# Tile 0 loaded in two halves on two queues, K of two tiles projected together, LayerNorm of tiles 2 and 3 skewed: an attention and gated-MLP kernel

## The chip, the cores and the metric

The kernel runs on one core of one Trainium2 chip. The metric is the device time of one execution in microseconds (us). Executions of one kernel spread by about 1 us here, so every verdict rests on several rounds in which two kernels run in turn on the same chip. The span that a profile shows is about 2 us shorter than the timed run.

A core has engines with instruction queues of their own: TensorE (PE, with PEld for its weight loads), VectorE (DVE), ScalarE (ACT), GpSimd (POOL) and SyncE (SP), which in this kernel only issues transfers. Transfers ("DMA") are issued on SP's, ACT's or POOL's queue.

## The reference

```python
x = A_x                                   # 1 x 2048 x 640, bf16
xn = _layernorm(x)
return x + _A_ref(xn, A_wqkv, A_wo) + _B_ref(xn, B_w_gate, B_w_up, B_w_down)

# A: q, k, v = split(xn @ wqkv), 32 heads of 20; each position attends to 8 earlier
#    positions 2 apart; softmax; the weighted sum of v; @ wo
# B: ((xn @ w_gate) * (xn @ w_up)) @ w_down, inner width 1536
```

## The kernel before

Rows are worked in 16 tiles of 128 (tile t holds rows 128t to 128t+127), the width of 640 in 5 chunks of 128. A small scheduler, `op(engine, fn, r=, w=)`, appends to the engine's queue in program order and derives all semaphore waits from what is read and written. So **the order of the calls is the order of each engine's queue**, and an instruction that waits holds up all that stand behind it.

The first four tiles are normalised and transposed on TensorE through PSUM. From tile 4 on SP issues a transposing DMA. The parts that the change touches:

```python
# loads: SP's queue unless eng says otherwise
op("act", ... ACT.Sqrt ..., name="sqrt_preload")
x_load(1, "act")
x_load(0)
for c in range(NCH):
    wqkv_load(0, c)                 # Q weights by chunk, 160 KB each
x_load(2)
x_load(3)
for c in range(NCH):
    wqkv_load(1, c)                 # K weights by chunk
...                                 # tiles 4 to 12

def ln_aggr(t):                     # cut: bn_aggr on DVE, then the square root on ACT
    op("dve", ... bn_aggr(mv, st) ...)
    op("act", ... activation(sd, mv[:, 1:2], ACT.Sqrt, bias=EPSC[:, 0:1]) ...)

def ln_sums(t, k):                  # tile 1's statistics, all on ACT: sum, sum of squares, square root
    ...

def ln_apply(t, between=None):      # cut: reciprocal and (x - mean) * rstd on DVE
    ...
    if t >= NTP:                    # NTP = 4
        op("sp", lambda e: e.dma_start_transpose(o, xs), ...)

def ln_copy(t, only=(0, 1, 2)):     # PSUM to XNT after the transposes: (engine, from chunk, to chunk)
    parts = ((("act", 0, 1), ("dve", 1, 3), ("act", 3, NCH)), (("dve", 0, 2), ("act", 2, NCH)), ...)[t]
    ...

warm(10)                            # dummy matmuls of 512 columns
ln_stats_a(0)
ln_stats_b(0)
ln_sums(1, 0)
ln_aggr(0)
ln_sums(1, 1)
ln_sums(1, 2)
ln_apply(0)
ln_pe(0)                            # five transposes
ln_copy(0, (0, 1, 2))
ln_apply(1)
warm(2, TS)
...
# projections of tiles 0 and 1: Q(0), Q(1), K(0), K(1), chunk by chunk; part_evac moves the result to SBUF on ACT
order = ((0, 0), (0, 1), (1, 0), (1, 1)) if t0 < 4 else ((0, 0), (1, 0), (0, 1), (1, 1))
at = {(0, 0): (3, lambda: tr(1)), (1, 0): (3, lambda: tr(2)), (1, 1): (4, lambda: tr(3))}
for which, dt in order:
    ...
    proj_tile(which, t, b, bm, (2 * which + t) * TS, at.get((which, t)))
    part_evac(which, t, 1, 0, 4, b, 0)
    tp += 1.4
    ...
    ln_pace(tp)                     # one more tile's LayerNorm each 1.45 us of planned time
```

Of the kernel before, what the change touches and what calls it, by code (L numbers as in the profile page):

```python
# [10 lines left out]
D = 640  # L11
NCH = 5
# [9 lines left out]
TS = 128  # L22
JB = 512
DHALF = D // 2
# [188 lines left out]
def build_kernel(nc, A_x, A_wqkv, A_wo, B_x, B_w_gate, B_w_up, B_w_down, out):  # L213
    K = Sched(nc)
    op = K.op
# [50 lines left out]
    XST = sb("XST", [128, NXS, D], at=a_log)  # L266
# [22 lines left out]
    xhbm = A_x[0]  # L289
    ohbm = out[0]  # L290

    def dma(o, i, r=(), w=(), name="", eng="sp", group=None):
        return op(eng, lambda e: e.dma_start(o, i), r=r, w=w, dma=True, name=name, group=group)
# [7 lines left out]
       r=[IDENT[:]], w=[IDENT[:]], name="ident")  # L301
# [7 lines left out]
    def x_load(t, eng="sp"):  # L309
        dma(XST[:, t % NXS, :], xhbm[t * TS:(t + 1) * TS, :], w=[XST[:, t % NXS, :]], name=f"xld{t}", eng=eng)  # L310
# [10 lines left out]
        dma(dst, wqkv_src[:, cs, g * D:(g + 1) * D], w=[dst], name=f"ld_wqkv{g}_{c}", eng=eng)  # L321

    op("act", lambda e: e.activation(DUM[:, 0:1], EPSC[:, 0:1], ACT.Sqrt), r=[EPSC[:]], w=[DUM[:]], name="sqrt_preload")
    x_load(1, "act")
    x_load(0)
    for c in range(NCH):
        wqkv_load(0, c)
    x_load(2)
# [11 lines left out]
    def late_loads():  # L340
        dma(MASK[0:128:4], MSK0[0:32], r=[MSK0[0:32]], w=[MASK[0:128:4]], name="mask")
        wqkv_load(2)
        for T, src in ((WG, B_w_gate), (WU, B_w_up)):
            for c in range(NCH):
                dma(T[:, c], src[c * 128:(c + 1) * 128, :], w=[T[:, c]], name="ld_w")

    def down_loads():
        dma(WD[:], B_w_down.rearrange("(c p) n -> p c n", p=128), w=[WD[:]], name="ld_wd")
# [15 lines left out]
    def ln_stats_a(t):  # L364
        if t >= NT:
            return
        x, st = XST[:, t % NXS, :], STATS[:, t % 2, 0:12]
        op("dve", lambda e: e.bn_stats(st[:, 0:6], x[:, 0:DHALF]), r=[x], w=[st], name=f"bna{t}")

    def ln_stats_b(t):  # L370
        if t >= NT:
            return
        x, st = XST[:, t % NXS, :], STATS[:, t % 2, 0:12]
        op("dve", lambda e: e.bn_stats(st[:, 6:12], x[:, DHALF:D]), r=[x], w=[("stb", t)], name=f"bnb{t}")

    def ln_aggr(t):
        if t >= NT:
            return
        st, mv, sd = STATS[:, t % 2, 0:12], MV[:, t, 0:2], SD[:, t, 0:1]
        op("dve", lambda e: e.bn_aggr(mv, st), r=[st, ("stb", t)], w=[mv], name=f"bnag{t}")  # L380
        op("act", lambda e: e.activation(sd, mv[:, 1:2], ACT.Sqrt, bias=EPSC[:, 0:1]), r=[mv, EPSC[:]], w=[("sd", t)],
           name=f"sd{t}")

    def ln_sums(t, k):
        x, xs, mv, sd = XST[:, t % NXS, :], XNS[:, t % NXN, :], MV[:, t, 0:2], SD[:, t, 0:1]
        nm, ss = mv[:, 0:1], mv[:, 1:2]
        if k == 0:
            op("act", lambda e: e.activation(xs, x, ACT.Copy, scale=-1.0 / D, accum_out=nm), r=[x], w=[xs, ("nm", t)], name=f"sta{t}")
        elif k == 1:
            op("act", lambda e: e.activation(xs, x, ACT.Square, bias=nm, accum_out=ss), r=[x, ("nm", t)], w=[xs, ("ss", t)],  # L390
               name=f"stq{t}")
        else:
            op("act", lambda e: e.activation(sd, ss, ACT.Sqrt, bias=EPSC[:, 0:1], scale=1.0 / D), r=[("ss", t), EPSC[:]],
               w=[("sd", t)], name=f"sd{t}")

    def ln_rstd(t):
        if t >= NT:
            return
        sd, rstd = SD[:, t, 0:1], SD[:, t, 1:2]
        op("dve", lambda e: e.reciprocal(rstd, sd), r=[("sd", t)], w=[("rstd", t)], name=f"rstd{t}")  # L400

    def ln_apply(t, between=None):
        if t >= NT:
            return
        x, xs, mv = XST[:, t % NXS, :], XNS[:, t % NXN, :], MV[:, t, 0:2]
        sd, rstd = SD[:, t, 0:1], SD[:, t, 1:2]
        op0 = ALU.add if t == 1 else ALU.subtract
        mean = ("nm", t) if t == 1 else mv
        if between is None:
            ln_rstd(t)  # L410
        else:
            between()
        for c0, c1 in ((0, 128), (128, D)) if t == 0 else ((0, D),):
            o, i = xs[:, c0:c1], x[:, c0:c1]
            op("dve", (lambda o, i: lambda e: e.tensor_scalar(o, i, mv[:, 0:1], rstd, op0=op0, op1=ALU.mult))(o, i),
               r=[i, mean, ("rstd", t)], w=[o], name=f"lnap{t}")
        if t >= NTP:
            o = XNT[:, :, t * TS:(t + 1) * TS]
            op("sp", lambda e: e.dma_start_transpose(o, xs), r=[xs], w=[o], dma=True, name=f"xT{t}")
        if t == 7:  # L420
            x_load(13)
            x_load2(14)
        if t == NT - 1:
            late_loads()

    def ln_pe(t):
        for c in range(NCH):
            o = tp_view(t, c, c + 1)[:, 0, :]
            i = XNS[:, t % NXN, c * 128:(c + 1) * 128]
            op("pe", (lambda o, i: lambda e: e.transpose(o, i, IDENT[:]))(o, i), r=[i, IDENT[:]], w=[o], name=f"tr{t}_{c}")  # L430

    def ln_copy(t, only=(0, 1, 2)):
        parts = ((("act", 0, 1), ("dve", 1, 3), ("act", 3, NCH)), (("dve", 0, 2), ("act", 2, NCH)), (("act", 0, NCH),),
                 (("act", 0, NCH),))[t]
        for k, (eng, c0, c1) in enumerate(parts):
            if k not in only:
                continue
            o = XNT[:, c0:c1, t * TS:(t + 1) * TS]
            tpv = tp_view(t, c0, c1)
            if eng == "dve":  # L440
                op("dve", (lambda o, i: lambda e: e.tensor_copy(o, i))(o, tpv), r=[tpv], w=[o], name=f"xntcp{t}_{c0}")
            else:
                op("act", (lambda o, i: lambda e: e.activation(o, i, ACT.Copy))(o, tpv), r=[tpv], w=[o],
                   name=f"xntcp{t}_{c0}")

    def warm(n, wide=JB):
        z = ZERO[:, 0:1].to_broadcast([128, wide])
        for _ in range(n):
            op("pe", lambda e: e.matmul(PS[:, 5, 0:wide], ZERO[:], z, start=True, stop=True), r=[ZERO[:]], w=[PS[:, 5, :]],  # L449
               name="warm")  # L450


    bank_ring = list(range(6))

    def bank():
        b = bank_ring.pop(0)
        bank_ring.append(b)
        return b
# [27 lines left out]
            op("pe", (lambda o, l, x, st, sp: lambda e: e.matmul(o, l, x, start=st, stop=sp))(o, l, x, st, sp),  # L486
               r=[l, x], w=[o], name=f"pp{which}_{m}_{t}_{c}")

    def proj_tile(which, t, b, bm, col, at=None):
        for c in range(NCH):  # L490
            if at is not None and at[0] == c:
                at[1]()
            for m in range(NCH):
                o = PS[:, b, m * TS:(m + 1) * TS] if m < 4 else PS[:, bm, col:col + TS]
                l, x = wcols(which, c, m), XNT[:, c, t * TS:(t + 1) * TS]
                st, sp = c == 0 and m in (0, 4), c == NCH - 1 and m in (3, 4)
                op("pe", (lambda o, l, x, st, sp: lambda e: e.matmul(o, l, x, start=st, stop=sp))(o, l, x, st, sp),  # L497
                   r=[l, x], w=[o], name=f"pp{which}_{m}_{t}_{c}")

# [204 lines left out]
                xr_load(t + NXR)  # L704


    warm(10)
    ln_stats_a(0)
    ln_stats_b(0)
    ln_sums(1, 0)  # L710
    ln_aggr(0)
    ln_sums(1, 1)
    ln_sums(1, 2)
    ln_apply(0)
# [8 lines left out]
        ln_stats_a(t + 1)  # L723
        ln_apply(t)

    def tr(t):
        ln_pe(t)
        if t != 2:
            ln_copy(t)
        ln_stats_a(t + 1)  # L730
        ln_stats_b(t + 1)
        ln_aggr(t + 1)
        if t == 2:
            ln_copy(t)
        if t < 3:
            ln_apply(t + 1)

    n_ln = [4]
    t_ln = [12.6]

    def ln_pace(t):
        while t_ln[0] <= t and n_ln[0] < NT:
# [5 lines left out]
            n_ln[0] += 1  # L748
            t_ln[0] += 1.45

    tp = 6.8
    for t0 in (0, 2, 4):
        bm = bank() if t0 == 4 else None
        if t0 == 2:
            bank_ring[:] = [5, 0, 6, 7, 2, 1, 3, 4]
            bm = bank()
        order = ((0, 0), (0, 1), (1, 0), (1, 1)) if t0 < 4 else ((0, 0), (1, 0), (0, 1), (1, 1))
        at = {(0, 0): (3, lambda: tr(1)), (1, 0): (3, lambda: tr(2)), (1, 1): (4, lambda: tr(3))}
        for which, dt in order:
            t = t0 + dt  # L760
            b = bank()
            if t0 == 0:
                if bm is None:
                    bm = bank()
                proj_tile(which, t, b, bm, (2 * which + t) * TS, at.get((which, t)))
            else:
                proj_part(which, t, (0, 1), b, 0)
                proj_part(which, t, (2, 3), b, 2 * TS)
                proj_part(which, t, (4,), bm, (2 * which + dt) * TS)
            part_evac(which, t, 1, 0, 4, b, 0)  # L770
            tp += 1.4
            if (which, dt) == (1, 1):
                for u in (0, 1):
                    part_evac(u, t0, 2, 4, 1, bm, 2 * u * TS)
            ln_pace(tp)
    bank_ring[:] = [6, 7, 2, 3, 4, 5, 0, 1]
    for g in range(5):
        b = bank()
# [187 lines left out]
```

## Time and profile before

| | |
|---|---|
| time, first three runs | 254.79 us median (254.24 to 255.25) |
| span of the profile | 252.5 us |
| TensorE busy | 99% |
| dummy matmuls | 1.00 to 5.45 us |
| first transpose of real data | 5.36 us |
| first projection matmul | 6.18 us |
| tile 0 landed / tile 1 landed | 3.03 / 3.72 us |
| Q weight chunks 2, 3, 4 (counted from 0) landed | 6.25, 6.63, 7.08 us |

The first lines of the page of before: the span, and for each engine the busy us, its share of the span and the number of instructions.

```profile
span 252.5 us, 3929 instructions
...
PE 249.1 (99%) x1623; PEld 149.3 (59%) x1623; DVE 214.7 (85%) x251; ACT 114.8 (45%) x204; POOL 35.9 (14%) x44
```

The chain that ended last, from the page of before, by engine:

```profile
PE 99%; DVE 0%; issue 0%
```

And the table of waits for TensorE, whole: engine, line and what it writes, what it waited for, us in total, times, longest.

```profile
PE PS L449 <- DVE EPSC L297: 1.0, 1, 1.0
```

All three say one thing: TensorE is the bound and never waits once it has started. Only two things can save time then: less TensorE work, or an earlier start of the useful work behind the dummies. How that start comes about is in the timeline of before (start us, duration, engine, line, operation, written<-read, form, count, and in brackets the idle time before it with what ended it):

```profile
3.06 0.49 DVE L368 BATCH_NORM_STATS2 STATS<-XST 128x6 f32<-128x320 bf16 x1 [1.75 <-DMA XST<-in_A_x_dram]
...
3.74 0.74 ACT L388 ACTIVATE XNS<-XST 128x640 bf16<-128x640 bf16 x1 [1.50 <-DMA XST<-in_A_x_dram]
...
3.98 0.21 DVE L380 BATCH_NORM_AGGREGATE MV<-STATS 128x2 f32<-128x12 f32 x1
...
4.48 0.28 ACT L381 ACTIVATE SD<-MV,EPSC 128x1 f32<-128x1 f32 x1
...
4.79 0.17 DVE L400 RECIPROCAL SD<-SD 128x1 f32<-128x1 f32 x1 [0.61 <-ACT SD L381]
4.99 0.64 DVE L415 TENSOR_SCALAR XNS<-XST,MV,SD 128x128 bf16<-128x128 bf16 x2
...
5.36 0.87 PE L430 MATMUL PS<-IDENT,XNS 128*128 128x128 bf16 x5
...
5.80 0.26 ACT L443 ACTIVATE XNT<-PS 128x128 bf16<-128x128 bf16 x1
...
6.18 1.04 PE L497 MATMUL PS<-XNT,WQKV 128*128 128x128 bf16 x15
```

The statistics of tile 0 are done at 4.19, but the square root (ACT L381) starts at 4.48, because ACT is still at tile 1's sum (L388). Ending times of the loads are read from the DMA semaphores in the trace.

### The profile page before, as it was taken

What the parts mean: (1) busy time and instruction counts of PE and PEld (TensorE: products, weight loads), DVE (VectorE), ACT (ScalarE), POOL (GpSimd) and SP (SyncE); (2) the same over time, 40 slices, a digit from 0 to 9 for tenths busy, and PEclk for the clock granted to TensorE, in tenths of its full rate; (3) what the DMA queues carried; (4) which work ended last, traced back from release to release, by engine and by line L of the source; (5) the groups of instructions that cost most, each with busy time, mean ns of one, the idle gap of its engine ahead of it and who ended that gap; (6) DMA issues with size and microseconds to landing.
All of it is one profiled execution on the core that took longest, in us unless ns stands there. A gap on an engine that the chain in (4) does not pass through costs nothing.

```text
span 252.5 us, 3929 instructions
## 1 busy us (share of the span) xinstructions
PE 249.1 (99%) x1623; PEld 149.3 (59%) x1623; DVE 214.7 (85%) x251; ACT 114.8 (45%) x204; POOL 35.9 (14%) x44
## 2 busy tenths in 40 slices
PE   8999999999999999999999999999999999999996
PEld 3999855555544444444444457764445777777775
DVE  4799999999999854999999974999999999993221
ACT  6577775555555557555555553135555112112000
POOL 1000001044515430003411110100000010111000
DMA  6969889956677471536379940393000021330511
GB/s 195 330 144 175 120 217 373 280 116 120 122 145 125 83 139 29 201 132 124 57 137 319 435 108 6 37 348 55 0 0 0 3 28 24 55 44 10 104 52 53
DMA packets 25649, 31.84 MB, mean 126 GB/s; under 512 B 9856, under 2 KB 22144, under 8 KB 25600
## 3 DMA queue, kind: packets, MB, share of 16 engines
q1 hardware_dynamic: 19104, 22.07, 28.4%
q0 software_dynamic: 6240, 9.31, 23.1%
q8 instruction: 12, 0.20, 0.3%
q10 hardware_dynamic: 288, 0.23, 0.3%
q14 instruction: 5, 0.04, 0.0%
HBM read 14.42 MB, written 4.59 MB: 75 GB/s over the span
## 4 chain that ended last, share of the span: by engine, by line
PE 99%; DVE 0%; issue 0%
PE PS L643 41%; PE PS L674 29%; PE PS L471 17%; PE PS L486 4%; PE PS L497 2%; PE PS L504 2%; PE PS L449 2%; PE PS L430 1%; DVE FOUT L688 0%; DVE ZERO L296 0%; DVE EPSC L297 0%
## 5 line engine op out<-in xcount | busy, mean ns | idle before, releaser
L643 PE MATMUL PS<-XNT,WG 128*128 128x512 bf16 x240 | 59.6, 379 | 0.0
L643 PE MATMUL PS<-XNT,WU 128*128 128x512 bf16 x240 | 59.6, 379 | 0.0
L610 DVE TENSOR_TENSOR PVB<-VO,ATB 128x10240 f16<-128x10240 bf16 x8 | 43.9, 5486 | 0.1
L471 PE MATMUL PS<-XNT,WQKV 128*128 128x512 bf16 x200 | 43.3, 379 | 0.0
L674 PE MATMUL PS<-WD,HT 128*128 128x320 bf16 (+2 forms) x300 | 43.2, 294 | 0.0
L643 PEld LDWEIGHTS PS<-XNT,WU 128*128 128x128 bf16 x240 | 23.5, 98 | 28.3
L643 PEld LDWEIGHTS PS<-XNT,WG 128*128 128x128 bf16 x240 | 23.5, 98 | 28.1
L645 ACT ACTIVATE USX<-PS 128x512 bf16<-128x512 f32 x48 | 28.7, 597 | 22.2 <-PE PS L643 21.2
L674 PEld LDWEIGHTS PS<-WD,HT 128*128 128x128 bf16 x300 | 28.7, 98 | 11.0
L471 PEld LDWEIGHTS PS<-XNT,WQKV 128*128 128x128 bf16 x200 | 23.5, 118 | 19.5
L605 DVE TENSOR_TENSOR PVB<-PVB 128x5120 f16<-128x5120 f16 (+1 forms) x16 | 34.5, 2154 | 0.3
L538 POOL DMA_DIRECT2D LOG<-PE x24 | 21.7, 931 | 59.6 <-DMA LOG<-PE 59.6
L645 ACT ACTIVATE HT<-PS 128x512 bf16<-128x512 f32 x36 | 21.5, 597 | 16.7 <-PE PS L643 16.7
L683 ACT ACTIVATE FACC<-PS 128x640 f16<-128x640 f32 x12 | 8.5, 704 | 45.4 <-PE PS L674 45.4
L674 PE MATMUL PS<-WO,VO 128*128 128x320 bf16 (+2 forms) x165 | 27.1, 295 | 0.0
L674 PEld LDWEIGHTS PS<-WO,VO 128*128 128x128 bf16 x165 | 15.9, 98 | 6.0
L527 DVE TENSOR_TENSOR PP<-QH,KH 128x2048 f16<-128x2048 bf16 x16 | 19.1, 1216 | 0.0
L527 DVE TENSOR_TENSOR TMP<-QH,KH 128x2048 f16<-128x2048 bf16 x16 | 19.0, 1216 | 0.0
L532 DVE TENSOR_TENSOR PP<-PP,TMP 128x4096 f16<-128x4096 f16 x8 | 18.3, 2288 | 0.2
L688 DVE TENSOR_TENSOR FOUT<-PS,XR 128x320 bf16<-128x320 f32 (+2 forms) x9 | 4.1, 454 | 16.6 <-PE PS L674 16.6
L698 POOL DMA_DIRECT2D out_dram<-FACC x6 | 7.1, 1186 | 76.5 <-ACT FACC L683 76.5
L538 POOL DMA_DIRECT2D PE<-PP x8 | 8.7, 1090 | 60.7 <-DVE PP L533 60.7
(67 smaller groups left out, 229.5 us busy)
## 6 DMA issues: line engine op xcount, KB each, us to landing
PE<-PP POOLq DMA_DIRECT2D x8, 512.0 KB, 5.0
ATB<-LOG SPq DMA_DIRECT2D x8, 512.0 KB, 4.8
LOG<-PE POOLq DMA_DIRECT2D x24, 128.0 KB, 2.7
WG<-in_B_w_gate_dram SPq DMA_DIRECT2D x5, 384.0 KB, 6.2
WU<-in_B_w_up_dram SPq DMA_DIRECT2D x5, 384.0 KB, 12.4
WD<-in_B_w_down_dram SPq DMA_DIRECT2D x1, 1920.0 KB, 10.0
out_dram<-in_A_x_dram SPq DMA_DIRECT2D x1, 1920.0 KB, 9.4
out_dram<-FACC POOLq DMA_DIRECT2D x6, 320.0 KB, 4.7
```

The costliest lines, as they stand in the source:

```text
L471: op("pe", (lambda l, x, c: lambda e: e.matmul(PS[:, b, :], l, x, start=(c == 0), stop=(c == NCH - 1)))(l, x, c), r=[l, x], w=[PS[:, b, :] ...
L486: op("pe", (lambda o, l, x, st, sp: lambda e: e.matmul(o, l, x, start=st, stop=sp))(o, l, x, st, sp), r=[l, x], w=[o], name=f"pp{which}_{m ...
L527: return (1.22, lambda: op("dve", lambda e: e.tensor_tensor(o, qw, kw, ALU.mult), r=[q, k], w=[o], name=f"prod{h}_{p}_{c}"))
L532: (2.3, lambda: op("dve", lambda e: e.tensor_tensor(a, a, b, ALU.add), r=[a, b], w=[a], name=f"psum{h}_{p}")),
L538: op("pool", lambda e: e.dma_start(o, i, accum_op=ALU.add), r=[o, i], w=[o], dma=True, name=name)
L605: return lambda: op("dve", lambda e: e.tensor_tensor(o, x, y, ALU.add), r=[x, y], w=[o], name=f"{name}_{b}")
L610: lambda: op("dve", lambda e: e.tensor_tensor(PVB[:], vw, aw, ALU.mult), r=[v, a], w=[PVB[:]], name=f"pv_{b}")),
L643: op("pe", (lambda l, x, c: lambda e: e.matmul(PS[:, b, :], l, x, start=(c == 0), stop=(c == NCH - 1)))(l, x, c), r=[l, x], w=[PS[:, b, :] ...
L645: op("act", lambda e: e.activation(o, PS[:, b, :], ACT.Copy), r=[PS[:, b, :]], w=[o], name=f"guev{which}_{m}_{j}")
L674: op("pe", (lambda l, x, i, b, wid: lambda e: e.matmul(PS[:, b, 0:wid], l, x, start=(i == 0), stop=(i == n - 1)))(l, x, i, b, wid), r=[l, ...
L683: op("act", (lambda o, i: lambda e: e.activation(o, i, ACT.Copy))(o, i), r=[PS[:, b - 1, :], PS[:, b, :]], w=[o], name=f"fin{t}")
L698: stores.append(op("pool", lambda e: e.dma_start(d, f, accum_op=ALU.add), r=[f, ("out",)], w=[("out", t)], dma=True, name=f"oacc{t}"))
```

## The change

The intent is an earlier start. Tile 0 comes in halves on two queues, so that its statistics can begin on the first half; the square root of tile 0 is queued ahead of tile 1's sum on ACT; the first copy goes to DVE; a dummy matmul is dropped. So that TensorE, running earlier, doesn't run into K weights that have not landed, K of tiles 0 and 1 is done chunk by chunk for both tiles. LayerNorm of tile 3 is started before tile 2's is finished. The loads of WG and WU become one transfer each.

```diff
+    for half, eng in ((0, "sp"), (1, "act")):
+        dst = XST[:, 0, half * DHALF:(half + 1) * DHALF]
+        dma(dst, xhbm[0:TS, half * DHALF:(half + 1) * DHALF], w=[dst], name=f"xh{half}", eng=eng)
     x_load(1, "act")
-    x_load(0)
     for c in range(NCH):
         wqkv_load(0, c)
 ...
-            for c in range(NCH):
-                dma(T[:, c], src[c * 128:(c + 1) * 128, :], w=[T[:, c]], name="ld_w")
+            dma(T[:], src.rearrange("(c p) n -> p c n", p=128), w=[T[:]], name="ld_w")
 ...        (bn_stats declare only the half that they read; lnap of tile 1 in two parts; cut)
-        parts = ((("act", 0, 1), ("dve", 1, 3), ("act", 3, NCH)), ...
+        parts = ((("dve", 0, 1), ("dve", 1, 3), ("act", 3, NCH)), ...
 ...        (proj_tile takes a list of tiles, chunk loop outside; cut)
-    warm(10)
+    warm(9)
     ln_stats_a(0)
     ln_stats_b(0)
+    ln_aggr(0)
     ln_sums(1, 0)
-    ln_aggr(0)
     ln_sums(1, 1)
 ...
+    def tr(t, c0=0):
+        ln_pe(t, c0)
+        ln_copy(t)
+        if t == 1:
+            ln_start(2)
+            ln_stats_a(3)
+            ln_stats_b(3)
+            ln_rstd(2)
+            ln_apply(2, lambda: ln_aggr(3))
-    t_ln = [12.6]
+    t_ln = [13.0]
 ...
+    bm = 1
+    proj_tile(0, [(0, 0)], bm, {(3, 3): lambda: ln_pe(1, 0, 2), (4, 1): lambda: tr(1, 2)})
+    part_evac(0, 0, 1, 0, 4, 0, 0)
+    proj_tile(0, [(1, 2)], bm)
+    part_evac(0, 1, 1, 0, 4, 2, 0)
+    ln_apply(3)
+    proj_tile(1, [(0, 3), (1, 4)], bm, {(3, 0): lambda: tr(2), (4, 0): lambda: tr(3)})
+    ln_start(4)
+    for t in (0, 1):
+        part_evac(1, t, 1, 0, 4, 3 + t, 0)
+    for u in (0, 1):
+        part_evac(u, 0, 2, 4, 1, bm, 2 * u * TS)
+    tp = 11.9
```

More of the change, by code (lines that the diff above doesn't have):

```diff
@@ L367, in ln_stats_a @@
         x, st = XST[:, t % NXS, :], STATS[:, t % 2, 0:12]
-        op("dve", lambda e: e.bn_stats(st[:, 0:6], x[:, 0:DHALF]), r=[x], w=[st], name=f"bna{t}")
+        op("dve", lambda e: e.bn_stats(st[:, 0:6], x[:, 0:DHALF]), r=[x[:, 0:DHALF]], w=[st], name=f"bna{t}")
     def ln_stats_b(t):
@@ L373, in ln_stats_b @@
         x, st = XST[:, t % NXS, :], STATS[:, t % 2, 0:12]
-        op("dve", lambda e: e.bn_stats(st[:, 6:12], x[:, DHALF:D]), r=[x], w=[("stb", t)], name=f"bnb{t}")
+        op("dve", lambda e: e.bn_stats(st[:, 6:12], x[:, DHALF:D]), r=[x[:, DHALF:D]], w=[("stb", t)], name=f"bnb{t}")
     def ln_aggr(t):
@@ L412, in ln_apply @@
             between()
-        for c0, c1 in ((0, 128), (128, D)) if t == 0 else ((0, D),):
+        for c0, c1 in {0: ((0, 128), (128, D)), 1: ((0, 256), (256, D))}.get(t, ((0, D),)):
             o, i = xs[:, c0:c1], x[:, c0:c1]
@@ L424, in ln_apply, with ln_pe @@
             late_loads()
-    def ln_pe(t):
-        for c in range(NCH):
+    def ln_pe(t, c0=0, c1=NCH):
+        for c in range(c0, c1):
             o = tp_view(t, c, c + 1)[:, 0, :]
@@ L432, in ln_copy @@
     def ln_copy(t, only=(0, 1, 2)):
-        parts = ((("act", 0, 1), ("dve", 1, 3), ("act", 3, NCH)), (("dve", 0, 2), ("act", 2, NCH)), (("act", 0, NCH),),
+        parts = ((("dve", 0, 1), ("dve", 1, 3), ("act", 3, NCH)), (("dve", 0, 2), ("act", 2, NCH)), (("act", 0, NCH),),
                  (("act", 0, NCH),))[t]
@@ L487, in proj_part, with proj_tile @@
                r=[l, x], w=[o], name=f"pp{which}_{m}_{t}_{c}")
-    def proj_tile(which, t, b, bm, col, at=None):
-        for c in range(NCH):
-            if at is not None and at[0] == c:
-                at[1]()
+    def proj_tile(which, tiles, bm, at={}):
+        for c, (t, b) in [(c, tb) for c in range(NCH) for tb in tiles]:
+            col = (2 * which + t) * TS
             for m in range(NCH):
+                if (c, m) in at and t == tiles[0][0]:
+                    at[c, m]()
                 o = PS[:, b, m * TS:(m + 1) * TS] if m < 4 else PS[:, bm, col:col + TS]
                 l, x = wcols(which, c, m), XNT[:, c, t * TS:(t + 1) * TS]
-                st, sp = c == 0 and m in (0, 4), c == NCH - 1 and m in (3, 4)
+                st = c == 0 and (m == 0 or m == 4 and t == tiles[0][0])
+                sp = c == NCH - 1 and (m == 3 or m == 4 and t == tiles[-1][0])
                 op("pe", (lambda o, l, x, st, sp: lambda e: e.matmul(o, l, x, start=st, stop=sp))(o, l, x, st, sp),
@@ L724, in ln_next, with ln_start @@
         ln_apply(t)
-    def tr(t):
-        ln_pe(t)
-        if t != 2:
-            ln_copy(t)
-        ln_stats_a(t + 1)
-        ln_stats_b(t + 1)
-        ln_aggr(t + 1)
-        if t == 2:
-            ln_copy(t)
-        if t < 3:
-            ln_apply(t + 1)
+    def ln_start(t):
+        ln_stats_a(t)
+        ln_stats_b(t)
+        ln_aggr(t)
+    def tr(t, c0=0):
[7 more added lines that the diff above has]
+            ln_apply(2, lambda: ln_aggr(3))
     n_ln = [4]
-    t_ln = [12.6]
+    t_ln = [13.0]
     def ln_pace(t):
@@ L749, in ln_pace @@
             t_ln[0] += 1.45
-    tp = 6.8
-    for t0 in (0, 2, 4):
-        bm = bank() if t0 == 4 else None
-        if t0 == 2:
-            bank_ring[:] = [5, 0, 6, 7, 2, 1, 3, 4]
-            bm = bank()
-        order = ((0, 0), (0, 1), (1, 0), (1, 1)) if t0 < 4 else ((0, 0), (1, 0), (0, 1), (1, 1))
-        at = {(0, 0): (3, lambda: tr(1)), (1, 0): (3, lambda: tr(2)), (1, 1): (4, lambda: tr(3))}
-        for which, dt in order:
+    bm = 1
[11 more added lines that the diff above has]
+    tp = 11.9
+    bank_ring[:] = [5, 0, 6, 7, 2, 1, 3, 4]
+    for t0 in (2, 4):
+        bm = bank()
+        for which, dt in ((0, 0), (1, 0), (0, 1), (1, 1)):
             t = t0 + dt
             b = bank()
-            if t0 == 0:
-                if bm is None:
-                    bm = bank()
-                proj_tile(which, t, b, bm, (2 * which + t) * TS, at.get((which, t)))
-            else:
-                proj_part(which, t, (0, 1), b, 0)
-                proj_part(which, t, (2, 3), b, 2 * TS)
-                proj_part(which, t, (4,), bm, (2 * which + dt) * TS)
+            proj_part(which, t, (0, 1), b, 0)
+            proj_part(which, t, (2, 3), b, 2 * TS)
+            proj_part(which, t, (4,), bm, (2 * which + dt) * TS)
             part_evac(which, t, 1, 0, 4, b, 0)
```

## The prediction

> What bounds it now. TensorE. The page gives PE 99% of 252.5 us; the chain of waits is PE from 1.00 to 250.19 us with no wait for another engine inside; the table of waits has one PE entry, 1.0 us before the first warm-up matmul. DVE (85%), ACT (45%) and the DMA queues matter only where they decide when PE's useful stream starts: ten dummy matmuls fill 1.00 to 5.45 us, the first transpose starts at 5.36, the first projection matmul at 6.18. What is won there is won whole; nothing else can be.
>
> The opening (timeline): tile 0 lands at 3.03; bn_stats 3.06 and 3.47, aggregate 3.98 to 4.19, square root only at 4.48 because ACT is busy with tile 1's sum (3.74 to 4.58), reciprocal 4.79, normalisation 4.99, transpose 5.36; chunk 0's copy at 5.80, behind tile 1's square root on ACT.
>
> The change:
> 1. Halves on two queues: the first bn_stats about 0.2 us earlier (2.85), the second at its pitch of 0.41, about 3.27. The Trainium skill ("DMA: Bandwidth & Descriptors", Specifications) asks for 512 B or more per transfer at line rate; 640 B rows keep that; no run here shows it yet. Tile 1 lands about 0.3 us later.
> 2. Tile 0's square root ahead of tile 1's sum: removes 0.25 us. With 1, the first transpose comes about 0.4 us earlier (4.95), as nine dummies end (1.00 + 9 x 0.427 = 4.84).
> 3. Chunk 0 copied on DVE: avoids ACT, whose tile 1 sums end about 0.45 us later.
> 4. Not all of the 0.4 stays. The matmul records show a pitch of 107 ns (128 columns) until 6.04 us and 56 ns after. The skill ("TensorE: Matmul & The Clock Gate", Part 1) explains it by a free-running activity window; the trace agrees in the halving, and the moment should not move with the kernel: work pulled ahead of it runs at half rate. Also, the Q weight chunks land at 6.25, 6.63 and 7.08 us whatever happens (same bytes ahead; DMA share 0.9 to 1.0 from 2 to 14 us in the table of stretches). After 7.15, eight matmuls and transposes of 0.056 remain of tile 0's Q: it ends about 7.6 instead of 7.89. Gain 0.25 to 0.3 us.
> 5. K by chunk: same 50 matmuls. K chunks land at 8.39, 8.84, 9.27, 10.07, 10.65; needed at 9.04, 9.6, 10.2, 10.7, 11.5: no stall, where tile by tile chunk 3 would wait 0.2 us. Keeps the gain, adds none.
> 6. Skewed LayerNorm: tiles 2 and 3 normalised near 10.1 and 10.8, before their transposes at 10.7 and 11.6. Neutral. Q evacuations move to about 10, behind tile 3's square root; their banks are not wanted until 12.4.
> 7. WG and WU as one load each: wanted at 72.6 (chain). Neutral.
>
> Prediction: 254.8 - 0.3 = 254.5 us, range 253.9 to 255.0 (before's runs spread by 1.0). Faster by over 2%: 1%; within 2%: 98%; slower: 1%.
>
> Right would show: first bn_stats near 2.85, square root near 4.0, first transpose near 4.95, no PE wait in the table of waits, tile 2's first Q matmul near 12.35 instead of 12.63. Wrong would be: first transpose after 5.2 (second half late on ACT's queue); PE idle before Q chunks 2 to 4 or before transposes of tiles 1 to 3; tile 5's transposed load late (landed 20.2, wanted near 20.8); or the clock rising later because PE idles between dummies and transposes.

## More of the kernel before

The issue lines of the first 2 us (written<-read, queue, count, KB each, median us from issue to landing) show tile 1 on ACT's queue:

```profile
WQKV<-in_A_wqkv_dram SPq DMA_DIRECT2D x2, 160.0 KB, 3.3
XST<-in_A_x_dram SPq DMA_DIRECT2D x1, 160.0 KB, 2.3
XST<-in_A_x_dram ACTq DMA_DIRECT2D x1, 160.0 KB, 2.7
```

## The result, and the profile after

The changed kernel takes 255.47 us (median of 6 runs, 254.87 to 255.98) against 254.50 for before (6 runs, 253.92 to 255.25). The ratio is 1.0037, 95% interval 1.0013 to 1.0061: slower by about 1 us, within 2%, and outside my range. (Ratios here are the mean time of one kernel's fast runs over that of the other's fast runs of the same rounds, so not quite the ratio of the medians quoted.) Timed again later beside other versions it was 254.89 (254.59 to 255.44) against 254.55, ratio 1.0014 (0.9995 to 1.0033). The loss is small, and only the first set is clear of noise by itself. What the trace shows is plainer than the time.

The page of after, span, busy times, and the chain that ended last by engine:

```profile
span 253.7 us, 3908 instructions
...
PE 248.4 (98%) x1607; PEld 149.4 (59%) x1622; DVE 214.7 (85%) x253; ACT 114.5 (45%) x203; POOL 35.9 (14%) x44
...
PE 89%; DMA 4%; DVE 3%; ACT 2%; issue 1%
```

The table of waits for TensorE, whole. Two lines are new:

```profile
PE PS L450 <- DVE EPSC L297: 1.0, 1, 1.0
PE PS L500 <- ACT XNT L444: 0.7, 1, 0.7
PE PS L472 <- DMA XNT<-XNS: 0.5, 1, 0.5
```

The timeline of the opening in after:

```profile
2.87 0.49 DVE L369 BATCH_NORM_STATS2 STATS<-XST 128x6 f32<-128x320 bf16 x1 [1.57 <-DMA XST<-in_A_x_dram]
...
3.79 0.21 DVE L381 BATCH_NORM_AGGREGATE MV<-STATS 128x2 f32<-128x12 f32 x1
...
4.04 0.29 ACT L382 ACTIVATE SD<-MV,EPSC 128x1 f32<-128x1 f32 x1 [1.79 <-DVE MV L381]
...
4.93 0.93 PE L431 MATMUL PS<-IDENT,XNS 128*128 128x128 bf16 x5
...
5.28 0.74 ACT L389 ACTIVATE XNS<-XST 128x640 bf16<-128x640 bf16 x1 [0.95 <-DMA XST<-in_A_x_dram]
...
5.87 1.14 PE L500 MATMUL PS<-XNT,WQKV 128*128 128x128 bf16 x15
...
7.10 0.29 ACT L394 ACTIVATE SD<-MV,EPSC 128x1 f32<-128x1 f32 x1
7.30 0.36 ACT L444 ACTIVATE XNT<-PS 128x256 bf16<-128x256 bf16 x1
...
7.63 0.64 DVE L416 TENSOR_SCALAR XNS<-XST,MV,SD 128x256 bf16<-128x256 bf16 x2
...
7.72 0.36 PE L500 MATMUL PS<-XNT,WQKV 128*128 128x128 bf16 x3 [0.71 <-ACT XNT L444]
...
8.03 0.29 PE L431 MATMUL PS<-IDENT,XNS 128*128 128x128 bf16 x2
```

What was meant to happen did happen: first statistics at 2.87 (predicted 2.85), square root at 4.04 (4.0), first transpose at 4.93 (4.95), first projection matmul at 5.87 instead of 6.18. Then tile 1's sum (ACT L389) starts only at 5.28, after 0.95 us of idling until its load landed: tile 1 has just come, at 5.26 instead of 3.72. Its square root ends near 7.4, the copy of tile 0's chunks 3 and 4 stands behind it on ACT (7.30), and TensorE waits. The issue lines of the first 2 us of after:

```profile
WQKV<-in_A_wqkv_dram SPq DMA_DIRECT2D x2, 160.0 KB, 3.4
XST<-in_A_x_dram ACTq DMA_DIRECT2D x1, 160.0 KB, 3.8
XST<-in_A_x_dram SPq DMA_DIRECT2D x1, 80.0 KB, 2.1
XST<-in_A_x_dram ACTq DMA_DIRECT2D x1, 80.0 KB, 2.2
```

Tile 1 now takes 3.8 us from issue to landing instead of 2.7, and was issued 0.4 us later (1.42 instead of 1.00).

The second wait is for a transposed tile, just as the 512-column projections begin. The timeline of SP in before, from 13 us on, the four transposing loads of tiles 4 to 7 and the two loads behind them:

```profile
14.20 5.86 SPq L419 DMA_TRANSPOSE XNT<-XNS  x4
20.10 1.05 SPq L293 DMA_DIRECT2D XST<-in_A_x_dram  x2
```

The same of after:

```profile
14.71 7.55 SPq L420 DMA_TRANSPOSE XNT<-XNS  x4
22.31 1.05 SPq L293 DMA_DIRECT2D XST<-in_A_x_dram  x2
```

TensorE's timeline at the change to 512 columns, in before:

```profile
29.31 2.54 PE L471 MATMUL PS<-XNT,WQKV 128*128 128x512 bf16 x11
```

The same of after:

```profile
30.79 1.03 PE L472 MATMUL PS<-XNT,WQKV 128*128 128x512 bf16 x4 [0.52 <-DMA XNT<-XNS]
```

The four transposing loads of tiles 4 to 7 keep SP for 5.86 us before and 7.55 after. The two loads behind them (tiles 13 to 15) start 2.2 us later, and so does the transposing load of tile 8. That of tile 11, the last of the four tiles which the first 512-column projections read, is issued 2.7 us later (27.79 instead of 25.09). Of that, 1.15 us are there when tile 5's load is issued (17.05 instead of 15.90); the rest is SP held longer, by the load of tile 6 alone for 2.54 us instead of 1.20.

The sum fits the spans. From the records of single matmuls, the fifteenth projection matmul starts at 7.00 before and at 6.79 after: 0.21 us won. Then the gap before the sixteenth is 0.93 us where the pitch is 0.06; tile 1's first transpose waits another 0.11; and 0.5 us are lost near 30.8. That is 0.87 + 0.11 + 0.5 - 0.21 = 1.27 us; the spans differ by 1.2 (253.7 against 252.5). Beyond 31 us TensorE waits for nothing in either trace. (15 matmul records are missing from the profile after, in long stretches one in each 50; so its busy time on PE, and small gaps, are not to be compared by the tenth.)

### The profile page after: what moved, and what is told of

The parts are those of the page before. It is cut to its first block, busy times and chain, and to the rows that moved or that the text cites. A ratio compares the mean times of both kernels' runs of the same rounds, so it can differ in the third digit from the quotient of the medians.

```text
span 253.7 us, 3908 instructions
## 1 busy us (share of the span) xinstructions
PE 248.4 (98%) x1607; PEld 149.4 (59%) x1622; DVE 214.7 (85%) x253; ACT 114.5 (45%) x203; POOL 35.9 (14%) x44
## 4 chain that ended last, share of the span: by engine, by line
PE 89%; DMA 4%; DVE 3%; ACT 2%; issue 1%
PE PS L646 41%; PE PS L677 29%; PE PS L472 17%; DMA XNT<-XNS 3%; PE PS L500 2%; DMA XST<-in_A_x_dram 2%; DVE STATS L369 1%; DVE STATS L375 1%; DVE XNS L416 1%; ACT KH L515 1%; PE PS L431 0%; ACT XNS L391 0%; ACT XNS L389 0%; ACT XNT L444 0%; ACT L323 0%
## 5 line engine op out<-in xcount | busy, mean ns | idle before, releaser
L646 PE MATMUL PS<-XNT,WG 128*128 128x512 bf16 x229 | 57.3, 379 | 0.6
```

Of the source, the lines that this page charges most:

```text
L646: op("pe", (lambda l, x, c: lambda e: e.matmul(PS[:, b, :], l, x, start=(c == 0), stop=(c == NCH - 1)))(l, x, c), r=[l, x], w=[PS[:, b, :] ...
```

## The experiments

I had three theories, and a fourth came from the first results.

- **L**: tile 1 is late because its load is now second on ACT's queue, behind the first weight chunks.
- **C**: what costs is ScalarE's order, the copy of chunks 3 and 4 behind tile 1's sums, as the table of waits names it.
- **J**: the joint K projection, with its burst of evacuations on ScalarE, costs the time, whatever the loads do.
- **F**: the wait near 30 us comes from stalls of SP's transposing loads while a 16 KB instruction fetch is in flight.

Each version computes the right result.

### 1. Tile 0 whole again, all else changed (e1_whole_tile0)

```diff
-    for half, eng in ((0, "sp"), (1, "act")):
-        ... two halves ...
     x_load(1, "act")
+    x_load(0)
```

> The changed kernel, with tile 0 loaded whole on SP and tile 1 first on ACT's queue, as before the change; all else changed. Theory L (tile 1's data come 1.5 us late because its load is now second on ACT's queue, behind the first weight chunks): tile 1 lands at 3.7 again, the square root of tile 1 near 6.1 instead of 7.10, no TensorE wait at 7 us (0.1 at most); 0.7 to 1.1 us faster than the changed kernel, so about the time of before, -0.2 to +0.2 us. Theory C (the copy of tile 0's chunks 3 and 4 stuck behind tile 1's sums in ScalarE's queue): nearly the same, as the sums end earlier. Theory J (the joint K and its burst of evacuations on ScalarE cost the time, whatever the loads do): the wait for a transposed load near 30 us stays, 0.4 us or more, and the kernel stays 0.4 us or more slower than before.

Measured: 254.60 us (254.17 to 254.76) against 254.37, ratio 1.0002 (0.9986 to 1.0018). Tile 1 landed at 3.61, its square root ran at 6.21, and the wait at 7 us was gone. The wait near 30 us stayed, as this line of its table of waits for TensorE says:

```profile
PE PS L470 <- DMA XNT<-XNS: 0.5, 1, 0.5
```

So L accounts for the first wait, and the second stays without tile 1's delay, as J said; whether for J's reason, experiments 4 to 8 ask. Theory J's time (0.4 us or more over before) did not come.

### 2. The halves alone, in the kernel before (e2_halves_alone)

```diff
 (kernel before)
-    x_load(1, "act")
-    x_load(0)
+    for half, eng in ((0, "sp"), (1, "act")):
+        ... two halves ...
+    x_load(1, "act")
     (bn_stats declare only the half that they read)
```

> The kernel before, with the two half loads of tile 0 alone (tile 1 second on ACT's queue). Theory L: tile 1 lands near 5.3; here its sum also stands in front of tile 0's square root on ScalarE, so the first transpose comes near 6.9 instead of 5.36 and the kernel is 1.2 to 1.8 us slower than before. Rival, as I predicted (halves delay tile 1 by 0.3 us only): within 0.2 us of before. Theory J: within 0.2 us of before.

Measured: 256.71 us (255.41 to 258.56) against 254.37, ratio 1.0091 (1.0058 to 1.0123): 2.3 us slower, more than L said. Tile 1 landed at 4.60, the square root of tile 0 behind its sum ran at 5.36, the first transpose at 6.24. The rest goes with the clock: TensorE had been idle for about 1 us after its dummies, and its matmuls kept the pitch of 107 ns until 10.0 us (6.0 in before). That the idling kept the clock down is likely, but this is one profile and no run tested it. The halves as loaded here harm by themselves; my figure of 0.3 us of delay is refuted.

### 3. The copy that TensorE waits for, on VectorE (e3_copy_on_dve)

```diff
-        parts = ((("dve", 0, 1), ("dve", 1, 3), ("act", 3, NCH)), ...
+        parts = ((("dve", 0, 1), ("dve", 1, 3), ("dve", 3, NCH)), ...
```

> The changed kernel, with the copy of tile 0's chunks 3 and 4 on VectorE, which is idle then, instead of ScalarE. The table of waits of the changed kernel names that copy for the 0.7 us wait. Theory C: the wait goes, 0.6 to 0.9 us faster than the changed kernel. Theory L: the copy is done by 6.4, but TensorE now waits for tile 1's normalised data instead, at its first transposes near 8.0, which do not move; the wait has another name and the time is the same within 0.1 us of the changed kernel, so 0.8 to 1.1 slower than before.

Measured: 255.00 us (254.91 to 255.31) against 254.37, ratio 1.0023 (1.0007 to 1.0038). The table of waits for TensorE in this version, without the line of the start:

```profile
PE PS L431 <- DVE XNS L416: 0.7, 1, 0.7
PE PS L472 <- issue: 0.2, 1, 0.2
```

The wait is as long as it was, 0.7 us, under another name: TensorE's transposes of tile 1 wait for the normalised tile. They start at 7.75 (8.03 in after; tile 1 landed at 4.98 in this run, 5.26 in after). C is refuted: the copy was only the first of two things held up by the same late tile. (The second line, put down to "issue", is the wait near 30 us: TensorE starts at 30.20, 0.3 us after tile 11 has landed.)

### 4. Tile 1 ahead of all weights (e4_tile1_ahead)

```diff
-    for half, eng in ((0, "sp"), (1, "act")):
-        ...
-    x_load(1, "act")
+    ... first half on SP, second half on ACT ...
+    x_load(1)                       # SP's queue, ahead of wqkv_load(0, c)
```

> The changed kernel with tile 1 loaded on SP's queue behind the first half and ahead of all weight chunks; second half alone on ACT's queue. Theory L: tile 1 lands near 3.5 to 3.8, its square root near 6.05, first transposes of tile 1 near 7.0 instead of 8.03, no TensorE wait at 7 us; 0.9 to 1.2 us faster than the changed kernel and 0.1 to 0.3 faster than before if the wait near 30 us goes with it. Theory J: that wait stays at 0.4 us or more, and the kernel is 0.2 us or more slower than before.

Measured: 254.56 us (254.22 to 254.94) against 254.37, ratio 1.0006 (0.9990 to 1.0021). Tile 1 landed at 3.63, its square root ran at 5.84, no wait at 7 us. L holds. The wait near 30 us is there, with 0.6 us, in its table of waits for TensorE:

```profile
PE PS L473 <- DMA XNT<-XNS: 0.6, 1, 0.6
```

That wait has a source of its own, then. ScalarE and VectorE show where it starts. ScalarE's timeline in the trace of experiment 4, after 13 us:

```profile
13.02 1.22 ACT L516 ACTIVATE KH<-PS 128x512 bf16<-128x512 f32 x2
14.14 0.38 ACT L516 ACTIVATE QH<-PS 128x256 bf16<-128x256 f32 x1
14.40 0.39 ACT L516 ACTIVATE KH<-PS 128x256 bf16<-128x256 f32 x1
14.67 0.62 ACT L516 ACTIVATE QH<-PS 128x512 bf16<-128x512 f32 x1
15.14 0.32 ACT L383 ACTIVATE SD<-MV,EPSC 128x1 f32<-128x1 f32 x1
```

VectorE's timeline in the same trace:

```profile
15.49 0.16 DVE L402 RECIPROCAL SD<-SD 128x1 f32<-128x1 f32 x1 [0.86 <-ACT SD L383]
```

Joint K brings four evacuations at once (2 x K, then Q and K of the last column block), and Q of tile 2 follows; the square root of tile 5 (L383, 15.14) stands behind all five, and VectorE sits idle for 0.86 us before its reciprocal. Tile 5's transposing load is issued at 16.17 (15.90 in before). But in before the same square root stood behind four of these evacuations already, as two lines of ScalarE's timeline in that trace show, the first evacuation and the square root:

```profile
13.39 0.59 ACT L512 ACTIVATE KH<-PS 128x512 bf16<-128x512 f32 x1
...
14.87 0.32 ACT L381 ACTIVATE SD<-MV,EPSC 128x1 f32<-128x1 f32 x1
```

So the joint K adds one evacuation in front of it and 0.27 us, while tile 11's load is issued 1.93 us later than in before (27.02 against 25.09). The rest, some 1.7 us, arises on SP behind tile 5: experiment 8 is about that.

### 5. The same, with LayerNorm from tile 4 on paced one step earlier (e5_tile1_ahead_pace)

```diff
 (on top of experiment 4)
-    t_ln = [13.0]
+    t_ln = [11.6]
 ...
     ln_start(4)
+    ln_pace(11.9)                   # statistics and square root of tile 5 ahead of the evacuations
     for t in (0, 1):
         part_evac(1, t, 1, 0, 4, 3 + t, 0)
```

> Tile 1 ahead of the weights, as in the run that had 0.6 us of wait left near 30 us, and in addition the LayerNorm of tiles 4 on paced one step earlier, so that the square root of tile 5 stands in ScalarE's queue ahead of the burst of four K and Q evacuations. Theory S (the burst delays that square root, and with it the chain of transposed loads, which SP issues one after another at 1.2 to 1.3 us each): the transposed load of tile 5 is issued near 15.0 instead of 16.17, tile 11's lands near 28.4 instead of 29.7, the wait near 30 us is gone (below 0.1), 0.4 to 0.7 us faster than without the pacing and 0.2 to 0.5 faster than before. Theory F (the wait comes from two stalls of SP's transposed loads, 0.7 and 0.95 us, while a 16 KB instruction fetch is in flight, and the queue's order has no part in it): the stalls stay, tile 11 lands 29.3 or later, wait 0.3 or more.

Measured: 254.43 us (254.20 to 255.64) against 254.36, ratio 1.0000 (0.9979 to 1.0020). Its table of waits for TensorE has no wait left but the one at the start:

```profile
PE PS L451 <- DVE EPSC L297: 1.0, 1, 1.0
```

And ScalarE's timeline in that trace, to be read against that of experiment 4:

```profile
13.46 0.29 ACT L383 ACTIVATE SD<-MV,EPSC 128x1 f32<-128x1 f32 x1 [0.34 <-DVE MV L382]
13.66 1.21 ACT L516 ACTIVATE KH<-PS 128x512 bf16<-128x512 f32 x2
```

The square root of tile 5 (13.46) is ahead of the evacuations, its transposing load is issued at 15.21 instead of 16.17, and tile 11's lands at 28.65 instead of 29.71, as S said of the trace. The time did not follow: neither the 0.4 to 0.7 us against experiment 4 nor the 0.2 us against before is visible. The long holds of SP stayed too (1.87 us for tile 7's load): tile 5's is issued 0.70 us earlier than in before, tile 11's still 0.22 us later. The pacing gave the chain a head start; it did not remove the holds.

### 6. The earlier pacing alone (e6_pace_alone)

```diff
 (changed kernel, loads as changed; pacing as in experiment 5)
```

> The changed kernel with the earlier pacing alone; loads as changed. If the two waits are separate: the wait near 7.7 us stays (0.8 to 0.9 us against the pitch), the one near 30 us goes; 0.4 to 0.6 faster than the changed kernel, so 0.3 to 0.7 slower than before. If the second wait only follows from the first: no gain over the changed kernel.

Measured: 255.28 us (254.81 to 255.71) against 254.36, ratio 1.0026 (1.0007 to 1.0045), as the theory of two separate waits said. The wait near 30 us is gone, the other is there, and longer (1.3 us in the table; tile 1 landed at 5.43, and TensorE ran ahead to it because its clock was up earlier in this run, at 4.6 us against 6.1). Against the changed kernel no gain can be read across the different rounds.

### 7. K tile by tile (e7_k_by_tile)

```diff
 (on top of experiment 4)
-    proj_tile(1, [(0, 3), (1, 4)], bm, {(3, 0): lambda: tr(2), (4, 0): lambda: tr(3)})
+    proj_tile(1, [(0, 3)], bm)
+    part_evac(1, 0, 1, 0, 4, 3, 0)
+    proj_tile(1, [(1, 4)], bm, {(1, 0): lambda: tr(2), (3, 0): lambda: tr(3)})
```

> Tile 1 ahead of the weights, and K of tiles 0 and 1 one tile after the other, with the evacuation of tile 0 right behind it; transposes of tiles 2 and 3 after as many matmuls as before. What I predicted of the joint K: tile by tile TensorE waits about 0.2 us for K chunk 3 near 10 us. Theory S: the burst on ScalarE is one evacuation shorter, tile 5's square root 0.4 to 0.6 us earlier, the wait near 30 us 0.2 to 0.6 us shorter. Net against the joint version: 0.0 to 0.4 faster. If joint K were needed: slower by 0.2 or more.

Measured: 254.77 us (254.68 to 255.49) against 254.36, ratio 1.0015 (0.9995 to 1.0035), not told apart from experiment 4. The trace shows two small gaps for K weights, 0.09 and 0.17 us over the pitch at 10.5 and 11.0 us; the prediction had 0.2. It also shows a wait of 0.8 us for a Q weight chunk at 7.3: the clock came up at 3.9 us in this run, TensorE was early, and chunk 3 landed at 7.15. As TensorE was late by that, the missing wait near 30 us proves nothing here (tile 5's load at 16.18, no earlier than in experiment 4). Whether joint K is worth having is left open.

### 8. The dummies narrow: 54 more TensorE instructions (e8_narrow_warm)

```diff
 (on top of experiment 4)
-    warm(9)
+    warm(36, TS)
```

> Tile 1 ahead of the weights, with the nine 512-column warm-up matmuls as 36 of 128 columns: same time, 54 more instructions for TensorE. Theory F (TensorE's instruction fetches of 16 KB, 256 instructions, stall the transposed loads): the fetches move earlier by 27 matmuls, 1.5 us at 128 columns and about 3 us at 256: from 17.2 to about 15.7 and from 25.6 to about 22.6; the transposed loads that take over 1.6 us to issue are now others (tile 5's, and tile 8's or 9's), not those of tiles 6 and 10. If the stalls have another cause (the number of the load, or data loads in flight), they stay at tiles 6 and 10. Time within 0.4 us of the version with nine.

Measured: 254.76 us (254.34 to 255.22) against 254.36, ratio 1.0010 (0.9985 to 1.0036). A transposing load keeps SP for 1.20 to 1.33 us as a rule. In experiment 4, tiles 6 and 10 took 1.92 and 2.23, with 16 KB instruction fetches in flight at 17.23 to 18.38 and 25.60 to 26.54 us. Between two such fetches TensorE runs some 250 instructions in the trace of before (184 between the first two, then 234 to 274). Here the fetches came at 16.25 to 17.29 and 23.80 to 24.93 (expected 15.7 and 22.6): tile 6 took 1.20, tile 10, which now was issued at 24.12, took 1.88, and all others the usual time. The first stall was gone, the second moved with the fetch to an earlier moment, though not to another tile. One thing speaks against F: the first fetch was in flight when tile 5's load was issued (16.48), and that load was not stalled, as F had expected. Tile 11 landed at 28.70, a whole us before experiment 4, and there was no wait near 30 us. (TensorE waited at other places, 0.6 us for tile 0's normalised data, as the narrow dummies ended early with the clock up at 3.8 us, and 0.2 us for a Q chunk; it reached its 512-column matmuls at 29.58, only 0.2 us later than in experiment 4 without the wait.) This supports F as a contribution, in part. Over all 14 traces, 533 packets of transposing loads took over 0.8 us between 14 and 34 us (18 ns is the rule), and 496 of them overlap a 16 KB fetch or the 0.4 us after it. That is a coincidence in time, if a close one, not a mechanism shown. In before the two fetches came at 17.92 and 24.86 and cost SP only 0.25 us (tile 7) and 0.6 (tile 11, the last that matters); in experiments 1 and 4 the first began 0.7 us earlier, at 17.2. Why SP is held longer in one case than in the other is not shown.

### 9 to 11. On one chip: the changed kernel, experiment 5 again, and tile 0 whole with the pacing

Experiment 11 is experiment 1 with the pacing of experiment 5. Nothing is edited in 9 and 10.

> The changed kernel unaltered, timed on the same chip as the three versions beside it. If its two waits are systematic, both are there again (0.7 to 1.6 us of gap near 7.7 us, 0.3 to 0.8 us near 30 us) and it is 0.7 to 1.2 us slower than before. If they were the luck of one profile: one or both are missing and the time is within 0.3 us of before.

> The version with tile 1 ahead of the weights and the earlier pacing, once more, for a finer interval: no wait near 7 us nor near 30 us. If my prediction's gain of 0.25 to 0.3 us is real once both waits are gone: ratio 0.9985 to 0.9995 to before, both sets of rounds together. If the gain is lost to the clock (matmuls ahead of the moment when it doubles run at half rate) and to the weight chunks: ratio 0.9995 to 1.0005.

> The changed kernel with tile 0 loaded whole and tile 1 first on ACT's queue as before, and the earlier pacing: all of the change but the halves, and no late square root of tile 5. No TensorE wait near 30 us (it was 0.5 us without the pacing). Against the version with tile 1 ahead and halves: 0.0 to 0.3 us slower, as its first statistics start 0.2 us later. Against before: -0.3 to +0.1 us.

| version | median us (range), 6 runs | ratio to before (95%) | waits of TensorE in its profile |
|---|---|---|---|
| before (11 runs) | 254.55 (254.10 to 255.32) | | none |
| 9, changed kernel | 254.89 (254.59 to 255.44) | 1.0014 (0.9995 to 1.0033) | 0.8 near 7.3, 0.3 near 30 |
| 10, tile 1 ahead, paced | 254.29 (254.03 to 254.47) | 0.9985 (0.9969 to 1.0000) | 0.3 near 7.3 (Q chunk 3) |
| 11, tile 0 whole, paced | 254.39 (254.10 to 254.49) | 0.9988 (0.9973 to 1.0003) | none |

Both waits of the changed kernel are there again, at about the lengths expected, so they are systematic; the 0.7 to 1.2 us expected of the time were too much, 0.3 to 0.4 was measured. All six runs of 10, and all six of 11, lie below all six of 9: the repaired versions are 0.65 to 0.73 us faster than the changed kernel (means 254.27 and 254.35 against 255.00). Against before, neither is clear of noise. Experiments 5 and 10, the same kernel, give 0.9990 (about 0.998 to 1.000) if weighted together by their intervals: inside the range expected of a real gain, but the interval holds both outcomes. Versions 10 and 11 don't differ visibly, so the halves themselves bring nothing that these runs can see.

### 12. The weights held back until tile 1 has landed (e12_weights_wait)

```diff
 (changed kernel; slower on purpose)
-        dma(dst, wqkv_src[...], w=[dst], ...)
+        dep = [XST[:, 1, :]] if (g, c) == (0, 0) else []
+        dma(dst, wqkv_src[...], r=dep, w=[dst], ...)
```

> The changed kernel, loads on the queues as changed, but the first weight chunk is not issued until tile 1 has landed (slower on purpose). It parts theory L in two: if sharing the DMA engines with the weight chunks makes tile 1 late, tile 1 now lands at 3.7 to 4.1 us instead of 5.0 to 5.4; if it is the second place on ACT's queue alone (issue at 1.43 instead of 1.01), it still lands at 4.9 or later. The weights come some 2 to 3 us later, so the time is 1.5 to 3.5 us over before, with TensorE waiting for weight chunks from about 6 us on.

Measured: 256.93 us, one run, 2.4 us over before. Of the issue lines of the first 2 us in this version, the one of tile 1:

```profile
XST<-in_A_x_dram ACTq DMA_DIRECT2D x1, 160.0 KB, 2.5
```

Same queue, same second place, same issue at 1.42 us, and 2.5 us to landing instead of 3.8: tile 1 landed at 3.97, against 5.26 in the profile of after. So of the 1.5 us by which it was late there, about 1.3 come from weight chunks in flight at the same time and 0.25 from the later issue, by this one profile. (In four more profiles with the loads as changed it landed at 4.60 to 5.43, 0.6 to 1.5 us after 3.97.)

## Why the prediction was wrong

**Right: the opening.** Points 1 and 2 for tile 0: statistics, square root and first transpose came within 0.04 us of the predicted times.

**Wrong, the step that failed: "Tile 1 lands about 0.3 us later" (point 1).** It landed 1.54 us later (5.26 against 3.72), 1.15 in the repeat (4.87). I counted the later issue and not the company. In before, tile 1 was issued at 1.00, ahead of all weights (the first chunk at 1.20), and its packets ran almost alone; issued at 1.42, with one chunk before it (1.20) and another each 0.47 us behind it (1.66, 2.14, ...), they share the transfer engines with the weights' packets: in the trace ACT's queue moved 135 KB of tile 1 between 2.5 and 3.0 us in before, and in the trace of after never over 59 KB in half a microsecond (88 in the repeat). The Trainium skill says as much: "DMA: Bandwidth & Descriptors", section "Queues, rings and completion order", has each transfer engine take turns between queues packet by packet, and "Trainium Kernel Development and Optimization", section "Key Constraints", says that transfers of SP, ACT and POOL all run on the same 16 engines and that several issuers only save issue time. Experiment 12 agrees with the first (2.5 us against 3.8). With the second agrees that tile 0 was complete at 2.85 to 3.36 us in the eleven traces where it came in halves on two queues, and at 2.99 to 3.03 in the three where it came whole. From this step the rest followed. Point 3 had tile 1's sums on ACT end 0.45 us later; the square root came at 7.10 instead of 5.60. Experiments 1 and 4 bring tile 1 back to 3.6 by two different ways, and both remove the wait; experiment 3 shows that the wait's name in the table (the copy) was not its cause.

**Wrong in part, a second step: "Skewed LayerNorm ... Neutral" (point 6), with "K by chunk ... adds none" (point 5).** I checked the banks and tiles 2 and 3, and named tile 5's load as a risk but only for its own use near 20.8. I did not follow SP's queue on to tile 11. It issues tiles 5 to 11 one after another at 1.2 to 1.3 us each, with the loads of tiles 13 to 15 between, and tile 11 is wanted as soon as the 512-column projections start: landed 28.34, wanted 29.31 in before. That is 1.0 us of slack, or 0.7 if one counts the 0.3 us that TensorE took to start after the landing wherever it waited. Without the late tile 1, a wait of 0.5 and 0.6 us was left (experiments 1 and 4). The traces give the shares. In these two, tile 5's load is issued 0.26 us later than in before, which is the net of all that the change did ahead of it, the burst of evacuations included; tile 11's load is issued 1.75 and 1.93 us later. The other 1.5 to 1.7 us come from SP being held longer, by tile 6 (1.87 and 1.92 us, 1.20 in before) and tile 10 (2.16 and 2.23, 1.28 in before), with a 16 KB fetch in flight each time. (It landed only 1.21 and 1.37 later, as in before tile 11 itself met a fetch.) So the delay that my point 6 overlooked could not have used up the slack by itself. The earlier pacing took the wait away wherever it was tried (5, 6, 10, 11), and so did shifting the fetches (8): against experiment 4 the first brought tile 11 in 1.06 us earlier, the second 1.02. Whether the change brought on the longer holds, by moving loads and fetches against each other, or they come by chance, stays open.

**Half right: "Not all of the 0.4 stays" (point 4).** The pitch halved near 6.0 us before and near 6.1 after. But the moment is not fixed from run to run, as I used it: in the profiles where TensorE was kept busy the half rate ended between 3.8 us (experiment 8) and 6.5 us (4 and 5). Nor did the Q chunks land at the same times "whatever happens": in after chunks 2 to 4 came at 5.75, 6.17 and 6.62, some 0.5 us earlier, with tile 1 now behind them. The skill's page ("TensorE: Matmul & The Clock Gate", Part 1) calls it run-variable, and the traces agree. That, and a Q chunk 3 that lands anywhere from 6.1 to 7.2 us, is where the hoped gain may have gone once both waits were cured: experiment 5's profile has no wait and starts its first 512-column matmul at 29.21 against 29.31 in before, 0.1 us won of the 0.25 to 0.3 predicted; in experiment 10's profile the Q chunk cost 0.3 us. An argued cause, not a shown one: no run held the clock's moment fixed, and the times of experiments 10 and 11 (by the means about 0.3 us under before, not clear of noise) leave open whether the gain was lost at all.

**Not seen: point 7.** WG and WU as one load each had no visible effect: TensorE waits for nothing after 31 us in the traces of before and after.

**The sum.** Predicted -0.3 us. The profile shows -0.2 for the earlier start, +1.0 for tile 1, +0.5 for tile 11: +1.3 against a span longer by 1.2 and a median later by 1.0.

## What to carry to other kernels

A load that is moved behind others pays for their bytes and not only for its issue slot: before splitting a transfer, list what else is in flight when the displaced one starts, and put the tile that a serial chain needs ahead of bulk weights. When a table names what was waited for, ask what that thing itself stood behind, and test it: moving the named copy moved the name and not the time. An engine that "has nothing to do with it" may issue a long chain of transfers one by one; follow the chain to its last member and compare its slack with every delay that the change puts at its head, and then read from the traces how much of the lateness came from the head and how much arose along the way.

## What the Trainium skill lacked or had wrong

- "DMA: Bandwidth & Descriptors" gives no issue time in us for a transposing load of this size. Here SP was held for 1.20 to 1.33 us by each one of 128 x 640 bf16 (SBUF to SBUF), and they landed 2.7 to 3.5 us (median of a trace) after their issue. In the traces of before and after SP issues tiles 8 to 11 with gaps of 0.04 us, so these holds set when tile 11 was issued.
- No page says that instruction fetches disturb transposing loads. In the traces here, 10 to 22 packets of 256 B, which take 18 ns as a rule, took 0.8 to 1.9 us while a 16 KB instruction fetch (itself 0.9 to 1.6 us) was in flight, and SP's issue of a transposing load was then up to 1.3 us longer (2.54 us in after). A coincidence in time; experiment 8 moved the fetches, and one of the two stalls of SP vanished, though with a fetch in flight.
- "DMA: Bandwidth & Descriptors" (Queues, rings and completion order) states the taking of turns between queues but gives no example of its price. Here: 160 KB on ACT's queue landed in 2.5 us with SP's queue held back and in 3.2 to 4.0 us beside weight chunks (five traces).
- "TensorE: Matmul & The Clock Gate" (Part 1) is right that the moment of the full clock varies; it puts the transition about 4 us into sustained work, give or take 0.5. Here, with dummies from 1.0 us on, it came from 3.8 to 6.5 us on the trace's axis, so 2.8 to 5.5 us into the work; and with about 1 us of idleness after the dummies it came at 10.0 us (experiment 2).
